# Infini-attention with an adaLN and a bilinear MLP: where ScalarE's bf16 copies, feature maps and high copies stand among the exponentials

## The chip, the cores and the metric

The kernel runs on one core of a Trainium2 chip. The metric is the device time of one execution in microseconds (us). Five engines work side by side, each on a queue of its own and in the order of that queue: TensorE (PE; its weight loads are listed apart as PEld), VectorE (DVE), ScalarE (ACT), GpSimd (POOL) and SyncE (SP), which issues the DMA transfers. An engine that waits for another holds up everything queued behind the waiting instruction.

## The reference

The input x has 2048 rows of 512. It is normed and modulated, goes through attention with 32 heads of 16 in four segments of 512 rows, is added back, and then goes through a second norm and a gated MLP of width 1376. Per segment:

```python
logits = einsum("bhqd,bhkd->bhqk", qs, ks) * scale + mask     # causal inside the segment
p = softmax(logits);  a_dot = einsum("bhqk,bhkd->bhqd", p, vs)
pq = phi(qs)                        # phi(t) = t + 1 where t > 0, exp(t) elsewhere
num = einsum("bhld,bhde->bhle", pq, M);  den = einsum("bhld,bhd->bhl", pq, z) + 1e-6
o = g * num / den + (1 - g) * a_dot
pk = phi(ks)
M = M + einsum("bhld,bhle->bhde", pk, vs);  z = z + pk.sum over l

x = x + ga * (o @ wo)
h = layernorm(x) * (1 + cb) + sb
x = x + gb * (((h @ w_gate) * (h @ w_up)) @ w_down)
```

All arithmetic is fp32. `sa, ca, ga, sb, cb, gb` come from silu(c) @ w_mod.

## The kernel before

**Stages.** A setup of some 45 us loads weights and makes the first segment's norm, k, q and v. The attention loop runs from about 45 to 545 us. The MLP stage takes the rest.

**Splitting for fp32.** Most products are made of three fp32r matmuls over a high and a low part of each operand: `wqH`, `wqL`, `ahH`, `ahL` and so on. A norm's output tile `hf` (in the profile `ahf` for the attention's norm, `chf` for the MLP's) is evicted from a PSUM bank by ScalarE (L183), ScalarE copies it into the high part (`ahH`, `chH`, L190) and POOL subtracts to get the low part (`ahL`, `chL`, L191). For the attention `hf` has two buffers, for the MLP one. The raw scores are made in bf16: k and q are cut into three bf16 parts (`q3`; in the profile `k` and `q`). Part 0 is a ScalarE copy (L657) with POOL's remainder `kr` or `qr` (L658); part 1 is a ScalarE cast of that remainder (L661), after which POOL makes part 2 (L662) and SyncE writes all parts to DRAM (`kd`, `qd`, L665 and L668), from where `load` reads them into `kst` and `qst`.

**The loop.** It steps over 32 units `v`, each of one segment, one of four groups of eight heads, and one half of the group: `u = s*8 + g*2 + half`. Five slots make a unit. A slot does this on TensorE, in this order: `q_step`, the raw scores of a coming unit into bank "lq", whose row maximum VectorE takes (`mxb`); pieces of the unit before, `av_step` (p times v) in slot 1 and `t_step` (transpose back, divide, add the memory's part into `orow`) in slot 4; `fill`, a share of background work; and `k_step`, the transposed scores into bank "lk", which ScalarE empties with one exponential into `pt` (L311), and POOL masks (L314). "lq" and "lk" have one buffer each, so the next `k_step` waits for the exponential before.

**Background work** is written as generators that yield after each piece. `fill_a` makes the coming segment: `ln` and the projections `a_kq` and `a_v`; `a_mem` is the memory's read and update of a group. `fill_b`, in the last segment, makes the output projection of the finished segments (`wo_op`: transposes `op`, high part `oH` by ScalarE, L421, low part `oL` by VectorE) and the MLP's first norm (`lnC`). `fill(share)` draws pieces from them until a credit of time is used up.

**a_kq** ends with the feature map phi, which is written as min(exp, 1) + relu: ScalarE makes `rl` (L681) and `e` (L682; `phk`, `phq` in the profile), and VectorE joins them in one min-and-add, which is put into the list `later` and issued by `flush()` in the next slot. `a_mem` transposes `phk` (bank `mp`, evicted as `pkr`, L720) and multiplies `phq` with the memory MZ (bank `up`, evicted as `us`, L731). `mp`, `up`, `mz` and `tr` share one bank, "sm".

**What sets the order.** TensorE's order is that of the program text: each matmul is chained behind the one before by a dependence without a semaphore. VectorE's instructions in the loop are chained in the same way. ScalarE, POOL and SyncE are ordered by the scheduler of the framework, which places each instruction as the program's dependences and its own model of time allow.

Of the kernel before, what the change touches and what calls it, by code (L numbers as in the profile page):

```python
# [57 lines left out]
def tile_kernel(ctx, tc, x, wq, wk_, wv, wo, beta, w_gate, w_up, w_down, c, w_mod, out):  # L58
    nc = tc.nc
# [19 lines left out]
    def pin(i):  # L79

        if last_pe[0] is not None:
            tc.add_manual_dep(i.ins, last_pe[0].ins.name, NOSYNC, reason="order")
# [4 lines left out]
    def TP(*a):  # L87
        return pe(nc.tensor.transpose(*a))
# [51 lines left out]

    def ln(pool, hpool, xt, s, sc, sh, pfx, hb, fast):

        first = pfx == "a" and s == 0
        V, A = (CV, CA) if first else (vec, act)
        mv = pool.tile([P, 4, 2], F32, tag="mv", name=f"{pfx}mv{s}", bufs=2)
        for t in range(4):
            st = pool.tile([P, 6], F32, tag="st", name=f"{pfx}st{s}_{t}", bufs=2)
            i = V.bn_stats(st, xt[t])  # L150
            if not first:
                pin(i)
            V.bn_aggr(mv[:, t, :], st)  # L153
            if not first:
                yield 0.0
        sd = pool.tile([P, 4], F32, tag="sd", name=f"{pfx}sd{s}", bufs=2)
        A.activation(sd, mv[:, :, 1], AF.Ln, bias=epst[:, 0:1])
        y = pool.tile([P, 4], F32, tag="y", name=f"{pfx}y{s}", bufs=2)
        A.activation(y, sd, AF.Exp, scale=-0.5)
        a = pool.tile([P, 4], F32, tag="ya", name=f"{pfx}ya{s}", bufs=2)  # L160
        b = pool.tile([P, 4], F32, tag="yb", name=f"{pfx}yb{s}", bufs=2)
        eng = CV if first else nc.gpsimd
        eng.tensor_mul(a, y, y)
        eng.tensor_scalar(b, mv[:, :, 1], 1.0, EPS, op0=ALU.mult, op1=ALU.add)  # L164
        eng.tensor_mul(b, b, a)
        eng.tensor_scalar(b, b, -0.5, 1.5, op0=ALU.mult, op1=ALU.add)
        eng.tensor_mul(y, y, b)
        yield 0.0
        for t in range(4):
            i = V.tensor_scalar(xt[t], xt[t], mv[:, t, 0:1], y[:, t:t + 1],  # L170
                                op0=ALU.subtract, op1=ALU.mult)
            if not first:
                pin(i)
                yield 0.0
        if first:
            yield 0.0
        hH, hL = [], []
        for d in range(KT):
            ps = bank(f"{pfx}tp{s}_{d}")
            for t in range(4):  # L180
                TP(ps[:, t * P:(t + 1) * P], xt[t][:, d * P:(d + 1) * P], ident)
            h = pool.tile([P, L], F32, tag="hf", name=f"{pfx}hf{s}_{d}", bufs=hb[2])
            A.activation(h, ps, AF.Identity, scale=sc[:, d:d + 1], bias=sh[:, d:d + 1])  # L183
            hi = hpool.tile([P, L], F32R, tag=hb[0].format(d), name=f"{pfx}hH{s}_{d}", bufs=hb[1])
            lo = hpool.tile([P, L], F32R, tag=hb[0].format(4 + d), name=f"{pfx}hL{s}_{d}", bufs=hb[1])
            if fast:
                V.tensor_copy(hi, h)
                V.tensor_sub(lo, h, hi.bitcast(F32))
            else:
                act.activation(hi, h, AF.Copy)  # L190
                nc.gpsimd.tensor_sub(lo, h, hi.bitcast(F32))  # L191
            hH.append(hi)
            hL.append(lo)
            yield 0.45
            if not first and d % 2 == 1:
                yield False
        return hH, hL

    def run(gen):
# [93 lines left out]
    def k_step(u, i):  # L293

        Q, K = qst[u % NB], kst[u % NB]
        kp = psp.tile([P, 2, 512], F32, tag="lk", name=f"k{u}_{i}", bufs=1)

        def mm(b, c, h, kb):
            MM(kp[:, b, c:c + L - kb * P], K[:, h, kb * P:(kb + 1) * P], Q[:, h, kb * P:], start=True, stop=True)

        for b in range(2):
            if i < 2:
                mm(b, 0, 2 * i + b, 0)
            elif i < 4:
                mm(b, 0, 2 * i - 4 + b, 1)
                mm(b, 384, 2 * i - 4 + b, 3)
            else:
                mm(b, 0, 2 * b, 2)
                mm(b, 256, 2 * b + 1, 2)
        pt = ap.tile([P, 2, 512], F32, tag="pt", name=f"pt{u}_{i}", bufs=PT)  # L310
        act.activation(pt, kp, AF.Exp, scale=0.25)  # L311
        v = pt.rearrange("p b (j t) -> p (b j) t", t=P)
        for w in ((v[:, 0:8:4],) if i < 2 else (v[:, 0:8:4], v[:, 3:8:4]) if i < 4 else (v[:, 0:8:2],)):
            sels[u, i] = nc.gpsimd.affine_select(w, w, pattern=[[0, w.shape[1]], [1, P]], compare_op=ALU.is_ge,  # L314
                                                 fill=0.0, base=0, channel_multiplier=-1)
        ptiles[u, i] = pt
# [308 lines left out]
            yield 0.68  # L625

    done = set()
    later = []

    def flush():  # L630

# [5 lines left out]
    def a_kq(s, g, nm):  # L637

        hH, hL = hcur[0]
        ph = phs.setdefault((s, g), {})  # L640
        if True:
            dst = kd if nm == "k" else qd
            ps = bank(f"{nm}ps{s}_{g}")
            n = 0
            for k in range(KT):
                for a, b in ((wH, hH), (wL, hH), (wH, hL)):
                    MM(ps, a[nm, g][:, k, :], b[k], start=n == 0, stop=n == 11)
                    n += 1
                    if n in (3, 6, 9):
                        yield 0.68  # L650
            f = pa.tile([P, L], F32, tag="f", name=f"{nm}f{s}_{g}", bufs=2)
            fast = s == 0 and g == 0
            A, V = (CA, CV) if fast else (act, nc.gpsimd)
            A.activation(f, ps, AF.Copy)
            q3 = pa.tile([P, 3, L], BF, tag="q3", name=f"{nm}3_{s}_{g}", bufs=2)
            r = pa.tile([P, L], F32, tag="qr", name=f"{nm}r_{s}_{g}", bufs=2)
            A.activation(q3[:, 0, :], f, AF.Copy)  # L657
            V.tensor_sub(r, f, q3[:, 0, :])  # L658

            def rest():  # L660
                (CV.tensor_copy if fast else act.copy)(q3[:, 1, :], r)  # L661
                V.tensor_sub(q3[:, 2, :], r, q3[:, 1, :])  # L662
                for r0, n, k in ((0, 3, 0), (3, 2, 0), (5, 1, 0)) if nm == "k" else ((0, 1, 3), (3, 1, 2), (5, 1, 1)):
                    if nm == "k":
                        nc.sync.dma_start(dst[s][g][r0:r0 + n].rearrange("r p t -> p r t"), q3[:, 0:n, :])  # L665
                    else:
                        i = 3 - k
                        nc.sync.dma_start(dst[s][g][r0:r0 + k].rearrange("r p t -> p r t"),  # L668
                                          q3[:, i:i + 1, :].to_broadcast([P, k, L]))

            if fast:
                rest()
            phi = (nm == "k" and s < NSEG - 1) or (nm == "q" and s > 0)
            if phi:
                if fast:
                    yield 0.0
                if nm == "q" and g > 0:
                    yield from drain()
                e = pa.tile([P, L], F32, tag="ph", name=f"ph{nm}{s}_{g}", bufs=3)
                rl = pa.tile([P, L], F32, tag="rl", name=f"rl{nm}{s}_{g}", bufs=1)  # L680
                act.activation(rl, f, AF.Relu)  # L681
                act.activation(e, f, AF.Exp)  # L682
                ph[nm] = e
            yield 0.68
            if not fast:
                rest()
            if phi:
                later.append(lambda: pin(vec.scalar_tensor_tensor(e, e, 1.0, rl, op0=ALU.min, op1=ALU.add)))
                if fast:
                    flush()  # L690
        nkq[s, g] = nkq.get((s, g), 0) + 1
        if nkq[s, g] == 2:
            done.add((s, g))
# [10 lines left out]
    def drain():  # L704
        while memq:
            w = mem_step()
            if w is not None:
                yield w

    def a_mem(s, g):  # L710

        ph = phs.pop((s, g))
        yield 0.0
        flush()
        if s < NSEG - 1:
            mp = pst((P, 512), "sm", f"mp{s}_{g}")
# [203 lines left out]
    run(av)  # L920
    btag[:] = ["ms"]
    vec.eng = CV
    share = (0.25, 0.0, 0.25, 0.25, 0.25)
    for v in range(-2, NQ + 1):
        rate[0] = 5.5
        on, prev = 0 <= v < NQ, 0 <= v - 1 < NQ
        for slot in range(5):
# [31 lines left out]
            fill(share[slot], slot < 4)  # L959
            if on:  # L960
                k_step(v, slot)
            if slot == 2 and 0 <= v + 1 < NQ:
                n_step(v + 1)
            if slot == 1 and 2 <= v + 3 < NQ:
                until((v + 3) // 8, (v + 3) // 2 % 4)
                load(v + 3)
    btag[:] = ["ms", "tb", "ms", "lk"]
    ps3 = [bank(f"wops3_{t}", shape=(P, 512)) for t in range(4)]
    for t in range(4):
# [98 lines left out]
```

## Time and profile before

| | us |
|---|---|
| median of 3 runs | 934.5 (934.47 to 936.42) |
| profiled execution, own time | 936.69 |
| its span | 934.9 |
| TensorE busy | 901.8 (96%) |
| VectorE busy | 470.9 (50%) |
| ScalarE busy | 409.1 (44%) |
| POOL busy | 313.6 (34%) |

The profiled execution's granted TensorE clock was 0.986 on average. Busy shares are averages over stages with different limits: in the MLP stage VectorE and ScalarE have little to do, and in the attention loop they are well occupied. The page's first lines give busy time by engine, its fourth part the chain of work that ended last, its fifth the costliest groups of instructions with the mean duration of one and the idle time before them. In the timeline a line has the start, the duration, the engine, the source line, the operation with its output and inputs, and in brackets the idle time before it and what ended that.

### The profile page before, as it was taken

To read this page: it belongs to the slowest core of one execution; us is meant where nothing else is said; L and a number is where in the kernel's file an instruction comes from. 1 tells how busy PE (TensorE), PEld (TensorE's weight loads), DVE (VectorE), ACT (ScalarE), POOL (GpSimd) and SP (SyncE) were. 2 spreads that over 40 slices of the span, in tenths; PEclk is the share of its full clock that TensorE was granted. 3 is DMA by queue.
4 is the path that set the end of the run, shared out by engine and by line. 5 is a ranking of instruction groups with operands and counts; after the bars stand their busy time and mean duration, and the time that the engine had idled before them with its cause. 6 is when DMAs were issued, how large, how long until landed. Compare 5 with 4: busy or idle time off the path is not lost.

```text
span 934.9 us, 14252 instructions
## 1 busy us (share of the span) xinstructions
PE 901.8 (96%) x5527; PEld 654.7 (70%) x5528; DVE 470.9 (50%) x758; ACT 409.1 (44%) x603; POOL 313.6 (34%) x455
## 2 busy tenths in 40 slices
PE   8998999999999999998999899999999999999997
PEld 6765666666666666665666668887888788878886
DVE  7577656686566856566667334652233223312112
ACT  3567757687576865577345612231112111211111
POOL 3175535566554763456414514551000000000000
PEclk8999999999999999999899999999999999999999
DMA  6584534655537543566762244440201020101011
GB/s 211 172 253 145 168 114 131 195 171 161 159 92 214 165 142 97 166 207 216 224 200 69 90 137 135 124 116 12 91 1 45 1 90 1 46 0 46 1 46 45
DMA packets 86211, 109.80 MB, mean 117 GB/s; under 512 B 9504, under 2 KB 58656, under 8 KB 86144
## 3 DMA queue, kind: packets, MB, share of 16 engines
q1 hardware_dynamic: 86000, 108.89, 37.6%
q8 instruction: 43, 0.70, 0.3%
q14 instruction: 24, 0.20, 0.1%
q10 hardware_dynamic: 144, 0.02, 0.0%
HBM read 67.98 MB, written 40.63 MB: 116 GB/s over the span
## 4 chain that ended last, share of the span: by engine, by line
PE 84%; DVE 6%; ACT 4%; DMA 3%; issue 1%; POOL 1%; DVEq 0%; SPq 0%; ACTq 0%
PE gps L1004 13%; PE ups L1004 13%; PE q L85 9%; PE tb L85 7%; PE k L85 7%; PE wops L85 5%; PE kps L85 4%; PE vps L85 4%; PE qps L85 3%; DVE mxb L39 2%; ACT pt L311 2%; PE acc0lq L1025 2%; PE acc2lq L1025 2%; PE acc3lq L1025 2%; PE acc1lq L1025 2%; PE acc1lk L1025 2%
## 5 line engine op out<-in xcount | busy, mean ns | idle before, releaser
L39 DVE TENSOR_REDUCE mxb<-q 128x8 f32<-128x1024 f32 x160 | 195.4, 1221 | 133.8 <-PE q L85 133.7
L311 ACT ACTIVATE pt<-k 128x1024 f32<-128x1024 f32 x160 | 163.6, 1022 | 81.0 <-PE k L85 79.6
L314 POOL TENSOR_SCALAR_AFFINE_SELECT pt<-pt 128x256 f32<-128x256 f32 (+1 forms) x224 | 98.9, 455 | 185.0 <-ACT pt L311 182.8
L1009 DVE TENSOR_TENSOR gs<-gs,ups 128x512 f32<-128x512 f32 (+1 forms) x44 | 30.2, 687 | 194.1 <-PE ups L1004 194.1
L85 PE MATMUL k<-qst,kst 98*128 98x384 bf16 (+3 forms) x512 | 98.0, 304 | 7.8 <-ACT pt L311 7.6
L85 PE MATMUL q<-kst,qst 96*128 96x128 bf16 (+2 forms) x640 | 96.7, 273 | 3.6 <-DVE mxb L39 2.3
L1008 ACT ACTIVATE gs<-gps 128x512 f32<-128x512 f32 (+1 forms) x44 | 26.1, 596 | 146.5 <-PE gps L1004 146.5
L1012 ACT ACTIVATE mH<-gs 128x512 fp32r<-128x512 f32 (+1 forms) x44 | 27.8, 633 | 130.5 <-DVE gs L1009 127.0
L85 PE MATMUL tb<-pt,v 128*32 128x512 f32 (+3 forms) x1024 | 75.5, 436 | 0.0
L85 PEld LDWEIGHTS <-kst 98*128 98x128 bf16 x512 | 38.5, 99 | 50.0 <-issue 44.3
L85 PEld LDWEIGHTS <-qst 96*128 96x128 bf16 x640 | 52.9, 98 | 28.1 <-issue 8.2
L1004 PE MATMUL gps<-chH,gH 128*128 128x512 f32 (+1 forms) x176 | 69.4, 394 | 0.0
L1004 PE MATMUL gps<-chH,gL 128*128 128x512 f32 (+1 forms) x176 | 69.3, 394 | 0.0
L1004 PE MATMUL ups<-chH,uH 128*128 128x512 f32 (+1 forms) x176 | 69.3, 394 | 0.0
L1004 PE MATMUL ups<-chL,uH 128*128 128x512 f32 (+1 forms) x176 | 69.3, 394 | 0.0
L1004 PE MATMUL gps<-chL,gH 128*128 128x512 f32 (+1 forms) x176 | 69.3, 394 | 0.0
L1004 PE MATMUL ups<-chH,uL 128*128 128x512 f32 (+1 forms) x176 | 69.2, 393 | 0.0
L85 PEld LDWEIGHTS tb<-pt,v 128*32 128x32 f32 x1024 | 28.7, 110 | 45.0 <-issue 40.4
L85 PE MATMUL q<-cmask,identb 128*128 128x128 bf16 (+1 forms) x320 | 54.6, 252 | 0.0
L164 POOL TENSOR_SCALAR cyb<-cmv 128x4 f32<-128x4 f32 x4 | 1.1, 275 | 143.5 <-DVE cmv L153 142.6
L1013 DVE TENSOR_TENSOR mL<-gs,mH 128x512 fp32r<-128x512 f32 (+1 forms) x44 | 31.7, 720 | 28.7 <-ACT mH L1012 28.5
L85 PEld LDWEIGHTS <-identb 128*128 128x128 bf16 x320 | 30.0, 98 | 17.2 <-issue 0.6
(267 smaller groups left out, 1843.8 us busy)
## 6 DMA issues: line engine op xcount, KB each, us to landing
kst<-kd SPq DMA_DIRECT2D x32, 384.0 KB, 4.5
qst<-qd SPq DMA_DIRECT2D x32, 384.0 KB, 5.2
wm<-in_w_mod_dram SPq DMA_DIRECT2D x24, 256.0 KB, 5.8
kd<-k SPq DMA_DIRECT2D x16, 384.0 KB, 4.1
qd<-q SPq DMA_DIRECT2D x16, 384.0 KB, 2.8
x<-in_x_dram SPq DMA_DIRECT2D x16, 256.0 KB, 4.9
kd<-k SPq DMA_DIRECT2D x16, 256.0 KB, 3.5
qd<-q SPq DMA_DIRECT2D x16, 256.0 KB, 3.7
```

The costliest lines, as they stand in the source:

```text
L39: i = getattr(self.eng, name)(*a, **k)
L85: return pe(nc.tensor.matmul(*a, **k))
L164: eng.tensor_scalar(b, mv[:, :, 1], 1.0, EPS, op0=ALU.mult, op1=ALU.add)
L311: act.activation(pt, kp, AF.Exp, scale=0.25)
L314: sels[u, i] = nc.gpsimd.affine_select(w, w, pattern=[[0, w.shape[1]], [1, P]], compare_op=ALU.is_ge, fill=0.0, base=0, channel_multiplier=-1)
L1004: nc.tensor.matmul(ps[0:n], a[:, k, 0:n], b[k], start=j == 0, stop=j == 11)
L1008: act.activation(gs[0:n], pss[0][0:n], AF.Copy)
L1009: vec.tensor_mul(gs[0:n], gs[0:n], pss[1][0:n])
L1012: act.activation(mH[0:n], gs[0:n], AF.Copy)
L1013: vec.tensor_sub(mL[0:n], gs[0:n], mH[0:n].bitcast(F32))
L1025: nc.tensor.matmul(acc[t], a[0:n, t * P:(t + 1) * P], b[0:n, :], start=i == 0 and j == 0, stop=i == NF - 1 and j == 2)
```

## The change

Inside the loop, ScalarE's instructions that empty no PSUM bank are no longer issued where the program text makes them. They become small functions in a queue `kept`: the high copy of a norm with POOL's subtraction (`parts`), part 0 of the bf16 parts with POOL's remainder (`part0`), the Relu (`phi0`), part 1 with POOL's part 2 and the writes to DRAM (`part1`), and the feature map's exponential (`phi1`), which also puts VectorE's min-and-add into `later`. After each slot's `k_step`, `give(2)` issues two of them, or three if more wait, each with a dependence (no semaphore) behind the slot's exponential, so that ScalarE's order has the exponential first. The whole queue is issued ahead of an eviction of `kf` or `qf`, ahead of a norm's eviction where more than one waits, at the end of a norm, ahead of each `load`, and at the end of the loop. `a_mem` issues one after another until the feature maps that it reads are made (`made`). In `a_kq` the draining of the memory's work moves ahead of the Relu. Outside the loop, and for the first group, all is issued at once as before.

```diff
+    kept, looped, lpt = [], [False], [None]
+    def keep(f):
+        if looped[0]:
+            kept.append(f)
+        else:
+            f()
+    def behind(i):
+        if lpt[0] is not None:
+            tc.add_manual_dep(i.ins, lpt[0].ins.name, NOSYNC, reason="order")
+        return i
+    def give(n=None):
+        n = len(kept) if n is None else n + (len(kept) > n + 1)
+        for _ in range(min(n, len(kept))):
+            kept.pop(0)()
...
     def ln(pool, hpool, xt, s, sc, sh, pfx, hb, fast):
...
+            if len(kept) > 1:
+                give()
             h = pool.tile([P, L], F32, tag="hf", name=f"{pfx}hf{s}_{d}", bufs=hb[2])
             A.activation(h, ps, AF.Identity, scale=sc[:, d:d + 1], bias=sh[:, d:d + 1])
...
-                act.activation(hi, h, AF.Copy)
-                nc.gpsimd.tensor_sub(lo, h, hi.bitcast(F32))
+                def parts(hi=hi, lo=lo, h=h):
+                    behind(act.activation(hi, h, AF.Copy))
+                    nc.gpsimd.tensor_sub(lo, h, hi.bitcast(F32))
+                keep(parts)
...
+        give()
         return hH, hL
...
     def k_step(u, i):
-        act.activation(pt, kp, AF.Exp, scale=0.25)
+        lpt[0] = act.activation(pt, kp, AF.Exp, scale=0.25)
...
     def a_kq(s, g, nm):
+            give()
             f = pa.tile([P, L], F32, tag="f", name=f"{nm}f{s}_{g}", bufs=2)
...
-            A.activation(q3[:, 0, :], f, AF.Copy)
-            V.tensor_sub(r, f, q3[:, 0, :])
+            def part0():
+                behind(A.activation(q3[:, 0, :], f, AF.Copy))
+                V.tensor_sub(r, f, q3[:, 0, :])
-            def rest():
-                (CV.tensor_copy if fast else act.copy)(q3[:, 1, :], r)
+            def part1():
+                if fast:
+                    CV.tensor_copy(q3[:, 1, :], r)
+                else:
+                    behind(act.copy(q3[:, 1, :], r))
                 V.tensor_sub(q3[:, 2, :], r, q3[:, 1, :])
...
+            if not fast:
+                keep(part0)
+            if phi and not fast and nm == "q" and g > 0:
+                yield from drain()
...
+            def phi0():
+                behind(act.activation(rl, f, AF.Relu))
+            def phi1():
+                behind(act.activation(e, f, AF.Exp))
+                made.add((s, g, nm))
+                later.append(lambda: pin(vec.scalar_tensor_tensor(e, e, 1.0, rl, op0=ALU.min, op1=ALU.add)))
...
+                for x in (phi0, part1, phi1) if phi else (part1,):
+                    keep(x)
...
     def a_mem(s, g):
+        while kept and any((s, g, nm) not in made for nm in ph):
+            give(1)
         flush()
...
+    looped[0] = True
     for v in range(-2, NQ + 1):
...
             if on:
                 k_step(v, slot)
+            give(2)
...
                 until((v + 3) // 8, (v + 3) // 2 % 4)
+                give()
                 load(v + 3)
+    give()
+    flush()
+    looped[0] = False
```

More of the change, by code (lines that the diff above doesn't have):

```diff
@@ L627, in tile_kernel @@
     done = set()
-    later = []
+    later, made = [], set()
     def flush():
@@ L669, in rest @@
                                           q3[:, i:i + 1, :].to_broadcast([P, k, L]))
-            if fast:
-                rest()
             phi = (nm == "k" and s < NSEG - 1) or (nm == "q" and s > 0)
+            if not fast:
+                keep(part0)
+            if phi and not fast and nm == "q" and g > 0:
+                yield from drain()
+            e = rl = None
             if phi:
[L675 to L678, printed above, removed]
                 e = pa.tile([P, L], F32, tag="ph", name=f"ph{nm}{s}_{g}", bufs=3)
                 rl = pa.tile([P, L], F32, tag="rl", name=f"rl{nm}{s}_{g}", bufs=1)
-                act.activation(rl, f, AF.Relu)
-                act.activation(e, f, AF.Exp)
-                ph[nm] = e
[L684 to L690, printed above, removed]
+            def phi0():
[4 more added lines that the diff above has]
+                later.append(lambda: pin(vec.scalar_tensor_tensor(e, e, 1.0, rl, op0=ALU.min, op1=ALU.add)))
+            if fast:
+                part0()
+                part1()
+                yield 0.0
+                if phi:
+                    phi0()
+                    phi1()
+                    flush()
+                yield 0.68
+            else:
+                for x in (phi0, part1, phi1) if phi else (part1,):
+                    keep(x)
+                if phi:
+                    ph[nm] = e
+                yield 0.68
+            if fast and phi:
+                ph[nm] = e
         nkq[s, g] = nkq.get((s, g), 0) + 1
@@ L965, in tile_kernel @@
                 until((v + 3) // 8, (v + 3) // 2 % 4)
+                give()
                 load(v + 3)
+    give()
+    flush()
+    looped[0] = False
     btag[:] = ["ms", "tb", "ms", "lk"]
```

## The prediction

> **What bounds the kernel now.** I read the page first: the span, then the chain that ended last.
>
> ```profile
> span 934.9 us, 14252 instructions
> ...
> PE 84%; DVE 6%; ACT 4%; DMA 3%; issue 1%; POOL 1%; DVEq 0%; SPq 0%; ACTq 0%
> ```
>
> TensorE (PE) carries 84% of the chain. ScalarE (ACT) carries 4%, and that small share is what the change can touch. So the question is where TensorE stands still because an exponential came late. The view of windows, over the attention loop (columns: stretch; length; busy time of PE, its weight loads, VectorE, ScalarE, POOL, each with its count; granted clock; DMA share; GB/s):
>
> ```profile
> 45.00:545.00 500.00, 476.20 (x3667) 314.26 (x3664) 320.18 (x492) 320.34 (x458) 259.86 (x379) 0.99 0.52 161
> ```
>
> TensorE is busy 476.20 of 500 us; all its idle time together is 23.8 us. ScalarE is busy 64% of the loop, so it has room on average, and order within a slot is all that can matter. The groups and the waits name the piece:
>
> ```profile
> L311 ACT ACTIVATE pt<-k 128x1024 f32<-128x1024 f32 x160 | 163.6, 1022 | 81.0 <-PE k L85 79.6
> ...
> PE k L85 <- ACT pt L311: 7.6, 12, 1.2
> ```
>
> There are 160 exponentials of 1.022 us. They usually wait for TensorE (79.6 us); TensorE waits for them 12 times, 7.6 us in all, because the bank "lk" that the exponential empties has one buffer. 7.6 us of 934.9 is the ceiling of what the change can give there: 0.8%. In about half of the twelve no deferrable part stands in front of the exponential, so the change cannot touch them; the four places below hold the rest.
>
> **The change, part by part: gains.** I compared the order of instructions on each engine before and after. TensorE's own order does not change. On ScalarE some forty exponentials go ahead of parts, but only where TensorE waited is that time. From the timeline (start, duration, engine; in brackets the idle time before and who ended it):
>
> ```profile
> 72.80 0.61 ACT L682 ACTIVATE phk<-kf 128x512 f32<-128x512 f32 x1
> 73.32 1.00 ACT L311 ACTIVATE pt<-k 128x1024 f32<-128x1024 f32 x1
> ...
> 74.37 0.59 PE L85 MATMUL k<-qst,kst 98*128 98x512 bf16 x2 [0.47 <-ACT pt L311]
> ...
> 90.53 0.63 ACT L190 ACTIVATE ahH<-ahf 128x512 fp32r<-128x512 f32 x1
> 91.07 1.00 ACT L311 ACTIVATE pt<-k 128x1024 f32<-128x1024 f32 x1
> ...
> 92.13 0.59 PE L85 MATMUL k<-qst,kst 98*128 98x512 bf16 x2 [0.57 <-ACT pt L311]
> ```
>
> At 73 us the exponential stood behind the 0.61 us feature map `phk`; in the new order it goes first, and the 0.47 us goes: take 0.5. At 91 us it stood behind the 0.63 us high copy `ahH`, which now follows it; of 0.57 I take 0.5.
>
> ```profile
> 204.21 0.60 PE L85 MATMUL k<-qst,kst 98*128 98x384 bf16 x4 [1.22 <-ACT pt L311]
> ...
> 206.27 1.45 ACT L183 ACTIVATE ahf<-atp,modc 128x512 f32<-128x512 f32 x2 [0.40 <-PE atp L88]
> ...
> 209.20 0.59 PE L85 MATMUL k<-qst,kst 98*128 98x512 bf16 x2 [0.66 <-ACT pt L311]
> ```
>
> At 201 to 209 us the waits are larger, 1.22 and 0.66, yet ScalarE itself is nearly full: its one gap in the stretch is 0.40, ahead of the evictions `ahf`. The new order puts the Relu, the exponential of the feature map and the second bf16 part (0.6 us each, as `phk` above) between the next exponential and those evictions, and the evictions free the banks for the transposes that follow. What the k matmul gains, the transposes hand back. Between 0 and 1.22 + 0.66 = 1.88 I take 0.2, below the 0.40 of slack.
>
> ```profile
> 330.96 1.45 ACT L183 ACTIVATE ahf<-atp,modc 128x512 f32<-128x512 f32 x2
> ...
> 332.82 1.02 ACT L311 ACTIVATE pt<-k 128x1024 f32<-128x1024 f32 x1
> 333.72 0.60 ACT L720 ACTIVATE pkr<-mp 128x512 f32<-128x512 f32 x1
> 333.89 0.60 PE L85 MATMUL k<-qst,kst 98*128 98x384 bf16 x4 [1.17 <-ACT pt L311]
> ...
> 334.98 0.45 PE L85 MATMUL up<-MZ,phq 128*128 128x136 f32 x2
> ```
>
> At 333 us the exponential loses the second eviction and a high copy in front, so the 1.17 us could go. What is late next is `pkr`: `up` needs the bank that `pkr` empties, `pkr` ends at 334.32 at the soonest (333.72 + 0.60), and `up`, moved up by 1.17, would want to start at 334.98 - 1.17 = 333.81. So 334.98 - 334.32 = 0.66 at most stays; I take 0.5. The gains sum to 0.5 + 0.5 + 0.2 + 0.5 = 1.7 us; in full as recorded the four places would give 0.47 + 0.57 + 1.88 + 1.17 = 4.1.
>
> **Losses.** The parts that move back feed POOL and VectorE, and these run in their own queues, where the late part finds something else in front. There are three places where TensorE then waits. First:
>
> ```profile
> 388.70 1.18 POOL L658 TENSOR_TENSOR kr<-kf,k 128x512 f32<-128x512 f32 x1
> 389.82 0.42 POOL L314 TENSOR_SCALAR_AFFINE_SELECT pt<-pt 128x256 f32<-128x256 f32 x1
> 389.92 0.62 ACT L661 CAST k<-kr 128x512 bf16<-128x512 f32 x1 [2.35 <-POOL kr L658]
> ```
>
> Here POOL's remainder `kr` comes behind one more select in the new order. ScalarE already stood 2.35 us for `kr` with the exponential queued behind the cast, so 0.42 more on POOL is 0.42 more for that exponential and the k matmul behind it: loss 0.4, from 0 to 0.42.
>
> The last of these lines is the group that the first belongs to (busy time, then mean ns of one).
>
> ```profile
> 426.01 0.68 DVE L39 SCALAR_TENSOR_TENSOR phq<-phq,rlq 128x512 f32<-128x512 f32 x1
> ...
> 427.71 1.22 DVE L39 TENSOR_REDUCE mxb<-q 128x8 f32<-128x1024 f32 x1 [0.18 <-PE q L85]
> ...
> 428.26 0.63 PE L85 MATMUL up<-MZ,phq 128*128 128x136 f32 x4
> 428.43 1.27 POOL L366 TENSOR_TENSOR orow<-orow,memb 128x512 f32<-128x512 f32 x1
> ...
> L39 DVE SCALAR_TENSOR_TENSOR phq<-phq,rlq 128x512 f32<-128x512 f32 x12 | 11.4, 949 | 0.0
> ```
>
> Second, the last unit's feature map: VectorE's min-and-add was done 1.57 us before `up` reads it at 428.26. In the new order it stands behind one more row maximum, the one at 427.71. It then ends at 427.71 + 1.22 + 0.68 = 429.61, and `up`, and all of TensorE behind it, starts 429.61 - 428.26 = 1.35 late. With the group's mean of 0.949 instead of 0.68 it is 1.62. The bound above is that VectorE starts only when POOL's addition to `orow` ends, at 429.70: 429.70 + 0.68 - 428.26 = 2.1. The bound below is 0, should VectorE find the part before that maximum. I take 1.35, since the part's own row says 0.68. A group whose mean lies 0.27 above this row's 0.68 fits a VectorE that is sometimes held. The Trainium skill (SBUF — State Buffer, section "SBUF: two separate sides") says that VectorE and GpSimd share one pair of ports, and that an operation of VectorE with two operands in SBUF against one of GpSimd that reads SBUF waits for the whole other instruction; by it the loss here is the 2.1 and the net of the sum 0.8 worse, and that mean above 0.68 is on its side.
>
> Third, the layer norm of the first MLP segment, which runs inside the last units. Its float tile `chf` has one buffer, so its links follow one another:
>
> ```profile
> 509.41 0.63 ACT L190 ACTIVATE chH<-chf 128x512 fp32r<-128x512 f32 x1
> 510.13 1.26 POOL L191 TENSOR_TENSOR chL<-chf,chH 128x512 fp32r<-128x512 f32 x1 [1.02 <-ACT chH L190]
> 510.62 1.02 ACT L311 ACTIVATE pt<-k 128x1024 f32<-128x1024 f32 x1 [0.58 <-PE k L85]
> 511.54 0.77 ACT L183 ACTIVATE chf<-ctp,modc 128x512 f32<-128x512 f32 x1
> ...
> 516.67 0.60 PE L88 MATMUL op<-ident,orl 128*128 128x128 f32 x4
> ...
> 518.16 0.78 ACT L183 ACTIVATE chf<-ctp,modc 128x512 f32<-128x512 f32 x1
> 518.30 0.69 DVE L39 TENSOR_TENSOR oL<-op,oH 128x512 fp32r<-128x512 f32 x1 [0.84 <-ACT oH L421]
> ...
> 518.99 0.83 PE L88 MATMUL op<-ident,orl 128*128 128x128 f32 x4 [1.72 <-ACT chf L183]
> ```
>
> The high copy `chH` moves from 509.41 to behind the exponential of 510.62, to 511.54, where the next `chf` starts now: 2.13 later. POOL's `chL` and the next `chf` wait for it in turn, so that `chf` starts at 511.54 + 2.13 = 513.67. Its copy, `chL` and the third `chf` take 0.77 + 0.63 + 1.26 + 0.78 = 3.44, to 517.1 without any further queueing. The changed kernel makes the first `op` transposes wait for that third `chf`: 517.1 against 516.67, 0.45 late or a little more. The second `op` no longer waits for the fourth `chf`, which was its 1.72 us; its bank is now the one that `oL` reads, and `oL` ended at 518.30 + 0.69 = 518.99, the same moment. So it moves with the first, plus what `oH` waits behind an exponential. I take 1.0 in all, between 0 (`oL` comes earlier now that ScalarE is free of that eviction) and 2.1 (the whole shift). The losses sum to 0.4 + 1.35 + 1.0 = 2.75.
>
> **Edits costed at nothing.** The bf16 remainders, and the writes of kd and qd on SyncE's queue that hang on them, come up to a slot later. Ahead of a load all queued parts are given out, so a load never passes its write.
>
> ```profile
> qst<-qd SPq DMA_DIRECT2D x32, 384.0 KB, 5.2
> ...
> 405.81 0.33 SPq L235 DMA_DIRECT2D qst<-qd  x1
> ...
> 418.88 0.38 PE L85 MATMUL q<-kst,qst 96*128 96x512 bf16 x1
> ```
>
> A load lands after 5.2 us and is read 418.88 - 405.81 = 13.1 us after its issue. That leaves 7.9 us of cover; without it the late write's delay, one exponential and a part, would be paid per unit. The MLP stage runs outside the loop and keeps its order: nothing.
>
> **The sum.** +2.75 - 1.7 = +1.05 us, made against the profiled execution: 936.7 of its own time, 934.9 of span and 1.8 around it. That execution lies 2.2 above the median of the runs shown, 934.5. The difference carries over: forecast 935.5. A measurement can tell about 0.2% from no change, 1.9 us, so this is "same".
>
> **Rivals.** Faster: the recorded waits come back in full, and the layer norm costs nothing since `op` is rid of its 1.72 us wait. Then 0.4 + 1.35 - 4.1 = -2.35, so 932.2; with the min-and-add early as well, 930.8. For it speaks that a mere change of order frees ScalarE at the exact places of the waits; against it that 206.27 shows only 0.40 of slack there.
>
> Slower: the parts that feed POOL and VectorE are the bound. The layer norm's one buffer passes its whole 2.1 on and the min-and-add waits for POOL, 2.1: 0.4 + 2.1 + 2.1 - 1.7 = +2.9, so 937.4. It decides for "slower" once these two cost 3.2 together, as 1.9 + 1.7 - 0.4 = 3.2. For it speaks `chf` with its 1.72 us wait already; against it that this wait's bank changes.
>
> The clock: the new waits fall together at 516 to 520 us.
>
> ```profile
> 517.00:520.00 3.00, 1.28 (x9) 0.80 (x8) 1.12 (x3) 2.70 (x5) 2.00 (x4) 0.89 0.07 10
> 520.00:523.00 3.00, 3.00 (x17) 2.81 (x16) 1.54 (x4) 2.06 (x3) 2.08 (x4) 0.54 0.85 315
> ```
>
> After 3 us in which TensorE was busy 1.28, the granted clock was 0.54 for the next 3 us: 3 x 0.46 = 1.4 us lost. Another such stretch, at 428 us say, gives 935.5 + 1.4 = 936.9. The Trainium skill (TensorE: Matmul & The Clock Gate, section "What's actually happening") has the clock halved after one idle window of about 3.4 us; by it the estimate is 1.7 us for a window, and the trace, which lost the clock with TensorE partly busy, bears it out only roughly.
>
> No effect: ScalarE's exponentials go first but every place is covered elsewhere: 934.5.
>
> **How the numbers follow.** Forecast 0.34 (own range 933.2 to 936.8, by the bounds of the two larger losses); faster 0.28; slower 0.25; the clock 0.08; no effect 0.05. Of the forecast's 0.34 I put 0.05 above +1.9. So slower is 0.25 + 0.08 + 0.05 = 0.38, the same 0.29 + 0.05 = 0.34, faster 0.28. As both signs hold much of the chance, the range reaches from near the faster case's end, 931.0, to the slower case with a part of the clock's price, 938.5.
>
> **What would show it.** The waits of k on pt should fall from 12 and 7.6 us to about 8 and 4 to 5, without one at 73, 92 and 333 us. `up` near 428 should wait for VectorE by 1 to 2 us, and `op` near 517 for `chf`, then for `oL`. If k's waits fall by less than 1.7 the gains were mis-sized; if new waits on POOL's remainders or on q and k loads appear elsewhere, a place was missed; a stretch at half clock near 428 or 392 decides for the clock.

## The result and the profile after

The changed kernel is slower, by 0.36%: a median of 938.4 us over 20 runs (935.7 to 943.2) against 935.3 for the kernel before over 20 runs of its own (932.75 to 938.4). The ratio is 1.0036, with a 95% interval of 1.0023 to 1.0049. The forecast was +1.05 us and "same"; the measured +3.1 to +3.4 us is outside what was called the same.

The page of the kernel after, span and chain:

```profile
span 938.3 us, 14251 instructions
...
PE 84%; DVE 9%; ACT 3%; DMA 2%; issue 1%; POOL 0%; SPq 0%; DVEq 0%; ACTq 0%
```

ScalarE's share of the chain fell from 4% to 3%, VectorE's rose from 6% to 9%. The waits show it in detail (who waited for whom: us in all, times, longest). First the kernel before, groups that the prediction did not quote:

```profile
PE op L88 <- DVE oL L39: 3.5, 3, 1.6
PE q L85 <- DVE mxb L39: 2.3, 4, 1.3
PE wops L85 <- DVE oL L39: 2.3, 3, 1.7
PE atp L88 <- DVE x L39: 2.0, 2, 1.0
...
PE mz L85 <- DVE orow L39: 0.4, 1, 0.4
```

and the kernel after:

```profile
PE op L88 <- DVE oL L39: 5.5, 4, 2.0
PE q L85 <- DVE mxb L39: 3.8, 9, 1.3
PE k L85 <- ACT pt L335: 3.4, 7, 1.2
PE atp L88 <- DVE x L39: 3.1, 3, 1.1
...
PE up L85 <- DVE phq L39: 1.4, 1, 1.4
...
PE mz L85 <- DVE orow L39: 1.0, 2, 0.7
...
PE wops L85 <- DVE oL L39: 0.6, 2, 0.4
```

k's waits for the exponential fell from 7.6 us to 3.4, by 4.2, and op's 1.7 us wait for `chf` shrank to a short one. In their place came op on `oL` (+2.0), q on `mxb` (+1.5), `up` on `phq` (+1.4), `atp` on `x` (+1.1) and `mz` on `orow` (+0.6): 6.6 us, all of them waits for VectorE. One wait for VectorE shrank, that of `wops` (the output projection's matmul) for `oL`, by 1.7.

The offset of the same TensorE instruction between the two traces (its start after minus its start before) shows where the 3.3 us of span arose. It is +0.80 at 43 us, before any queued part is issued; +1.24 at 390 us; +1.16 at 425 us and +2.74 at the `up` of 428 us; +1.73 at 451 us; +3.33 at the `wops` behind 523 us, where it stays to the end. So the first 350 us of the loop, with all four places of the predicted gain, brought +0.4 and no gain. The two late places brought +1.6 each. Between them, at 445 us, 1.0 came back, where TensorE had waited in the kernel before:

```profile
445.68 0.79 PE L85 MATMUL wops<-woH,oH 128*128 128x512 f32 x1 [1.73 <-DVE oL L39]
```

This is no gain of the change. The traces of late_now, last_now, ln_clean and before_fold below gain 0.8 to 1.4 us on the trace of before there too, and before_fold is the kernel before without one small product. The wait was long in this one execution of before.

### The profile page after: what moved, and what is told of

Read it like the earlier page. It is cut to its first block, busy times and chain, and to the rows that moved or that the text cites. A ratio compares the mean times of both kernels' runs of the same rounds, so it can differ in the third digit from the quotient of the medians.

```text
span 938.3 us, 14251 instructions
## 1 busy us (share of the span) xinstructions
PE 904.8 (96%) x5528; PEld 656.3 (70%) x5528; DVE 471.6 (50%) x758; ACT 407.8 (43%) x603; POOL 313.8 (33%) x455
## 4 chain that ended last, share of the span: by engine, by line
PE 84%; DVE 9%; ACT 3%; DMA 2%; issue 1%; POOL 0%; SPq 0%; DVEq 0%; ACTq 0%
PE ups L1057 13%; PE gps L1057 13%; PE q L85 9%; PE tb L85 7%; PE k L85 6%; PE wops L85 4%; DVE mxb L39 4%; PE vps L85 4%; PE kps L85 4%; PE qps L85 3%; PE acc2lq L1078 2%; PE acc0lq L1078 2%; PE acc3lq L1078 2%; PE acc1lq L1078 2%; PE acc1lk L1078 2%; PE acc0lk L1078 2%
## 5 line engine op out<-in xcount | busy, mean ns | idle before, releaser
L338 POOL TENSOR_SCALAR_AFFINE_SELECT pt<-pt 128x256 f32<-128x256 f32 (+1 forms) x224 | 96.8, 446 | 185.8 <-ACT pt L335 184.4
```

## The clock, and how the runs are compared

The +0.8 at the start is in the setup, which the change does not touch. These are windows of before and then of after (the granted clock is the third number from the right):

```profile
11.00:25.00 14.00, 13.93 (x67) 12.36 (x69) 11.53 (x25) 6.26 (x8) 0.00 (x0) 0.63 0.63 195
```

```profile
11.00:25.00 14.00, 14.00 (x61) 12.39 (x60) 9.42 (x21) 5.11 (x7) 0.00 (x0) 0.51 0.55 170
```

In the setup the clock was granted at half for 10.2 us in the one execution and 13.7 in the other, and in the execution of kq_only below for none. The mean clock varies from run to run of one kernel, and the time with it: the 20 runs of after lie near a line from 935.7 us at a mean clock of 0.992 to 943.2 at 0.979, and 80 runs of before near one from 930.2 at 0.998 to 938.0 at 0.982, about 0.4 to 0.6 us for each 0.001. Differences of 1 us drown in that. So beside each ratio I give the time at a clock of 0.986, read from a straight line through the kernel's own runs. It is a working of mine and good to about 1 us; for the kernels without `rd` and for those with halved row maxima, six runs each, it reads the line beyond all or most of their clocks. It also has a weakness: the mean clock holds the half-clock stretches that a change itself makes, so a part of their price is taken out. By it before is at 935.2 and after at 938.3: +3.0.

## Experiments

**Undoing the late places together.** Theory: the loss is the two late places, and the gains are handed back. Rival: bad luck with the clock, or a loss spread over the loop. In late_now these parts are issued at once:

```diff
-                keep(parts)
+                keep(parts, pfx == "c")
...
-                keep(part0)
+                keep(part0, last)
...
-                    keep(x)
+                    keep(x, last)
```

with `last = s == NSEG - 1 and g == NG - 1`, and `keep(f, now)` calling `f` at once where `now` holds.

> As after, but the parts of the last segment's last group and of the MLP's norm are issued at once. Theory A: the two late places are gone (1.5 us at 428 us, 1.7 us at 517 to 523 us), everything earlier stays as in after; 935.2, equal to before within 0.5 us, with k's waits on pt still at some 4 us instead of 7.6. Theory B or a loss spread over the loop: still 937.5 to 938.4.

Measured: 936.4, ratio 1.0010 (0.9994 to 1.0026), that is +0.9 us and between -0.6 and +2.4; at equal clock 935.3, 0.0 from before. Its waits:

```profile
PE q L85 <- DVE mxb L39: 3.5, 9, 1.3
PE op L88 <- DVE oL L39: 3.5, 3, 1.6
PE k L85 <- ACT pt L335: 3.2, 7, 1.0
PE atp L88 <- DVE x L39: 3.1, 3, 1.1
PE op L88 <- ACT chf L204: 1.7, 1, 1.7
```

The waits at the two places are those of before again, and k still waits only 3.2 us instead of 7.6: 4.4 us of k's waits are gone, and the time is not below that of before. The clock as the cause of the whole loss falls: the twelve runs of late_now had the same mean clock as those of after, 0.985, and were 2.0 us shorter by the medians, 2.4 by the ratios and 3.0 at equal clock.

**Undoing each by itself**, last_now and c_now, each with one half of that edit.

> As after, but the parts of the last segment's last group are issued at once; the MLP's norm stays queued. Theory: the wait of up on phq (1.4 us) goes, the op waits near 519 us stay: 936.9, 1.5 us below after and 1.6 above before. If the late places are worth nothing alone: 938.4.

> As after, but the MLP's norm issues its high copies at once; the last group stays queued. Theory: the op place costs what it costs before (1.7 us for chf and none for the second bank), up at 428 us still waits 1.4 us: 936.9 to 937.4, 1.0 to 1.5 us below after. If that place is covered (as ln_clean's 934.6 suggests): 938.4, level with after.

Measured: last_now 937.7, ratio 1.0041 (1.0022 to 1.0061), at equal clock 937.3; c_now 937.2, 1.0027 (1.0008 to 1.0045), at equal clock 937.4. By ratio last_now is a miss, no better than after, and c_now is 0.8 us below it; by equal clock each is about 1 us below after's 938.3. Their traces are plainer: in last_now `up` comes 1.4 us earlier than in after and never waits; in c_now the op place is back to 1.7 us and the half-clock stretch behind it ends 3.4 us sooner. c_now's waits on k, q, `atp` and `up` are those of after within 0.3 us. The intervals don't separate 1.0 from 1.5 us, so the size of each place alone rests on the traces, and on late_now for their sum.

**Queueing one kind of part.** kq_only calls `parts()` at once in the norms; ln_only calls the parts of a_kq at once. One piece of the edit of ln_only:

```diff
-                for x in (phi0, part1, phi1) if phi else (part1,):
-                    keep(x)
+                for x in (phi0, phi1, part1) if phi else (part1,):
+                    x()
```

> Only the bf16 parts and feature maps are queued; the norms' high copies are issued at once, as before the change. Theory A: the op waits near 519 us are again those of before, up at 428 us still waits 1.4 us for VectorE; 936.6, 1.3 us above before. Theory C (the norm's parts are the whole loss): at or below before, 934.5 to 935.3. A rival that puts all on the bf16 parts: 938.4.

> Only the norms' high copies are queued; the bf16 parts and feature maps are issued at once, as before the change. Theory A (two late places, gains handed back to VectorE): the wait of up at 428 us goes (1.4 us less than after), the waits of op near 519 us with the longer half-clock stretch stay; 936.8, that is 1.5 us above before. Theory B (the clock was unlucky in after's runs, no place of the change is at fault): within 0.5 us of before, as would kq_only. Theory C (the norm's parts, with their one buffer, are the whole loss): as slow as after, 938.4.

kq_only: 936.8, ratio 1.0017 (1.0001 to 1.0032), at equal clock 937.1; expected 936.6. ln_only: 945.2, ratio 1.0111 (1.0091 to 1.0132), where 936.8 was expected. This was a miss of the experiment, not of the norm: calling `phi1` at once puts VectorE's min-and-add into `later` a slot earlier than in either kernel, and VectorE then stands in its fixed order for a feature map that ScalarE has not made. The groups of ln_only in the loop (after the second bar the idle time before them, and who ended it):

```profile
L39 DVE SCALAR_TENSOR_TENSOR phq<-phq,rlq 128x512 f32<-128x512 f32 x12 | 11.2, 936 | 3.5 <-ACT phq L714 3.5
...
L39 DVE SCALAR_TENSOR_TENSOR phk<-phk,rlk 128x512 f32<-128x512 f32 x11 | 10.4, 943 | 7.6 <-ACT phk L714 7.6
```

and one line of its waits:

```profile
PE q L85 <- DVE mxb L39: 6.3, 10, 2.4
```

VectorE idles 11.1 us there, 0.3 to 0.4 in after, and q's wait for the row maxima behind it grows to 6.3 us. ln_clean repairs that: part 1 and the min-and-add stand where they stood before the change.

```diff
+                    phi0()
+                    act.activation(e, f, AF.Exp)
+                    ph[nm] = e
+                yield 0.68
+                part1()
+                if phi:
+                    made.add((s, g, nm))
+                    later.append(...)
```

> Only the norms' high copies are queued; the bf16 parts, the feature maps and VectorE's min-and-add are issued at the same points as before the change (ln_only gave the min-and-add to VectorE a slot earlier). Theory A: up at 428 us does not wait, the op waits near 519 us are those of after; 936.5. If the 10 us of ln_only belong to queueing the high copies: 945.

Measured: 934.6, ratio 1.0002 (0.9987 to 1.0017); at equal clock 935.2. The 10 us are gone, and the runs are 1.9 us better than the 936.5 expected (1.3 at equal clock). The op place has the waits of after:

```profile
511.85 0.85 PE L88 MATMUL op<-ident,orl 128*128 128x128 f32 x4 [0.54 <-ACT chf L204]
514.50 1.11 PE L88 MATMUL op<-ident,orl 128*128 128x128 f32 x4 [1.80 <-DVE oL L39]
```

Against before, a wait of 0.54 is added and 1.72 becomes 1.80, and the offset to before grows there by 1.7 us, as in after. The runs show no such loss: +0.2 us, between -1.2 and +1.6. Why they came out below what the trace shows is open. k's waits on pt are still 7.0 us in its loop: with the norms alone queued hardly any gain is made, and hardly any is handed back.

**What takes the gains back?** In two places of the trace of after VectorE is held by POOL where it was not, or less, before. At 178 us, in before:

```profile
177.14 0.17 DVE L39 TENSOR_TENSOR rd<-rd,omg 128x16 f32<-128x16 f32 x1
177.17 1.16 POOL L662 TENSOR_TENSOR k<-kr,k 128x512 bf16<-128x512 f32 x1
```

and in after:

```profile
177.11 1.28 POOL L692 TENSOR_TENSOR k<-kr,k 128x512 bf16<-128x512 f32 x1 [0.27 <-ACT k L691]
...
177.59 0.84 DVE L39 TENSOR_TENSOR rd<-rd,omg 128x16 f32<-128x16 f32 x1
...
178.46 0.42 DVE L39 TENSOR_TENSOR orow<-tr,rd 128x256 f32<-128x256 f32 x1
...
179.03 0.93 PE L85 MATMUL mz<-v,pkr 128*128 128x136 f32 x6 [0.70 <-DVE orow L39]
```

The same product of 128x16 takes 0.84 us instead of 0.17; it ends at 178.43, just behind POOL's part 2, which ends at 178.39. In before the product began 0.03 us ahead of part 2 and was not held; in after part 2 is first, since it comes no later than in before, and VectorE reaches the product 0.45 us later. `orow` follows, and TensorE's `mz`, which needs its bank, waits 0.70. The Trainium skill (SBUF — State Buffer, "SBUF: two separate sides") states this very hold for an operation of VectorE with two operands in SBUF beside one of GpSimd that reads SBUF: the one that starts first has the shared ports for its whole length. These starts and ends agree with it. So do the others in the two traces: 11 of these products took more than 0.25 us in before and 15 in after, and each of them ended 0.03 us behind an instruction of POOL. To take the victim away, the inverse of the factor (1-g) was put into the ones column of v, set once, so that the reciprocal gives the scaled value and the product goes:

```diff
+        nc.gpsimd.tensor_copy(a[:, 0:H * VS].rearrange("p (h e) -> p h e", e=VS)[:, :, DH], iom)
...
+        nc.gpsimd.tensor_mul(hmg[:, g, :, DH], hmg[:, g, :, DH], omg[:, g * HG:(g + 1) * HG])
...
         vec.reciprocal(rd, tr[:, :, :, DH])
-        og = omg[:, g * HG + h0:g * HG + h0 + 4]
-        vec.tensor_mul(rd, rd, og.unsqueeze(1).to_broadcast([P, 4, 4]))
```

> As after, with the factor (1-g) moved from VectorE's small product rd into the ones column of v (set once), so that the product with two operands in SBUF goes: 31 operations with a mean of 0.58 us leave VectorE. Theory A with VectorE held by POOL as the taker of the gains: the waits of mz on orow (1.0 us) and part of those of atp on x (3.1 us) and of q on mxb (3.8 us) go; 936.2, 2.2 us below after. Rival (rd's held time is off the path): 938.4, within 0.5 us of after.

> As before, with the factor (1-g) folded into the ones column of v, so that VectorE's product rd goes. Theory A (VectorE and POOL holding each other lies on the path, more so after the change): in before 1.1 us of TensorE's waits are for orow, so the gain is small here, 1.0 us; 934.3 beside 935.3. Rival (the fold is worth the same in both kernels, it has nothing to do with the change): 2.7 us or more below before, as the fold brought in after.

> As after, with both takers undone: the parts of the last group and of the MLP's norm are issued at once, and rd is folded away. Theory A: the two effects add up, 2.0 (late_now against after) + 2.7 (after_fold against after) = 4.7 us below after: 933.7, some 1 to 1.5 us below before and no slower than before_fold. Rival (the gains in k's waits are never real, since VectorE's row maxima pace the loop): level with before_fold or above it.

Measured: after_fold 934.8, ratio 1.0007 (0.9988 to 1.0025), by the ratios 2.7 us below after, where 2.2 were expected. But before_fold is at 930.1, ratio 0.9944 (0.9929 to 0.9959): the fold is worth 5.2 us by ratio (4.5 at equal clock) where I had said 1.0. late_fold is at 929.8, 0.9947 (0.9931 to 0.9962), level with before_fold. So the part of my theory that made this hold the special taker of the change's gains falls: the fold helps before more than after. `rd`'s groups, before and after, show that it was long in both:

```profile
L39 DVE TENSOR_TENSOR rd<-rd,omg 128x16 f32<-128x16 f32 x31 | 15.1, 486 | 1.1
```

```profile
L39 DVE TENSOR_TENSOR rd<-rd,omg 128x16 f32<-128x16 f32 x31 | 18.0, 580 | 1.1
```

The change added 2.9 us to 15.1; 31 products of 0.17 us would be 5.4. And without the product the gains still don't appear: before_fold has 8.4 us of k's waits in the loop and late_fold 3.4, in equal time. First before_fold, then late_fold:

```profile
PE k L85 <- ACT pt L310: 8.4, 13, 1.2
...
PE q L85 <- DVE mxb L39: 1.8, 2, 1.3
```

```profile
PE q L85 <- DVE mxb L39: 4.0, 9, 1.3
...
PE k L85 <- ACT pt L334: 3.4, 8, 1.0
```

5.0 us of k's waits went, and 2.2 us of waits of q for the row maxima came, on 7 more occasions. What is left of the 5.0 does not show in the medians, which are good to about 1 us. That gave the next theory: VectorE's row maxima take the gains. At 73 us, in after:

```profile
74.15 1.19 DVE L39 TENSOR_REDUCE mxb<-q 128x8 f32<-128x1024 f32 x1
...
74.50 0.61 PE L85 MATMUL k<-qst,kst 98*128 98x512 bf16 x2
...
75.39 0.61 PE L85 MATMUL q<-kst,qst 96*128 96x128 bf16 x8 [0.29 <-DVE mxb L39]
```

k no longer waits, and the q behind it does, because bank "lq" is still being read until 75.34. Halving the columns that a row maximum reads (a softmax keeps its value under another maximum) tests this:

```diff
-        vec.tensor_reduce(o, src, axis=AX.X, op=ALU.max)
+        vec.tensor_reduce(o, src[:, :, :, 0:64], axis=AX.X, op=ALU.max)
```

> As before, but each row maximum reads only the first half of each block of 128 columns (the other half is left out of the maximum), so that VectorE's 160 reductions last some 0.7 us instead of 1.22. Theory A' (the four gains are handed back because TensorE, once it need not wait for an exponential, stands at the next q matmul for VectorE's row maximum): waits of q on mxb (2.3 us) go, k's waits on pt stay at 7 us or grow; 932, 2 us below before.

> As after, with the halved row maxima. Theory A': the waits of q on mxb (3.8 us) go, up at 428 us waits 0.5 us less, the op place stays; 932.5, 5 to 6 us below after, and level with before_half because the two late places still cost what the gains bring. Rival (the handing back does not hang on the row maxima): 3 us above before_half, as after is above before.

> As late_now, with the halved row maxima. Theory A': the gains of k's waits show at last: 929.5, 2.5 us below before_half. Rival (VectorE's row maxima are not the taker): level with before_half within 1 us, as late_fold was with before_fold.

Measured: before_half 924.3, ratio 0.9899 (0.9870 to 0.9928); after_half 926.3, 0.9914 (0.9888 to 0.9939); late_half 923.7, 0.9877 (0.9851 to 0.9904). The size was missed by far: 0.53 us less in each row maximum is worth some 10 us of time, where 2 were expected. The waits on the maxima alone don't account for it. About half may be the hold by POOL: with shorter maxima VectorE comes to `rd` at other moments, and in before_half it is hardly held, where taking `rd` away had been worth 5.2 us:

```profile
L39 DVE TENSOR_TENSOR rd<-rd,omg 128x16 f32<-128x16 f32 x32 | 6.2, 195 | 1.1
```

No run separates the two. The comparison of the three does not settle the theory either: late_half lies 0.6 us under before_half by medians, where 2.5 were expected and the rival said less than 1; it is 1.7 at equal clock, and the intervals overlap. after_half lies 2.0 above before_half by medians, where the theory said level and the rival 3. The traces decide it place by place. The same place in after_half:

```profile
70.62 0.69 DVE L39 TENSOR_REDUCE mxb<-q 128x8 f32<-128x512 f32 x1
...
71.57 0.61 PE L85 MATMUL k<-qst,kst 98*128 98x512 bf16 x2
72.01 0.61 PE L85 MATMUL q<-kst,qst 96*128 96x128 bf16 x8
```

Here q follows k without a wait, and the 0.6 us that k gained on before_half is still there 70 us later. It is so at every such place. Between 43 and 390 us the offset falls at six k matmuls in either pair of traces. From before to after these gains sum to 4.3 us, and the very next q hands back 2.2 of them. From before_half to after_half they sum to 4.1, and the next q hands back 0.03. So the row maximum is shown as the taker of about half of what k gains.

The rest goes to other queues. At 317 us of after_half `atp` waits 0.8 us for VectorE's `x` where k had gained 0.8, and at 172 us `mz` waits 0.7 for `orow`. From 62 to 390 us after_half gains 1.1 us on before_half, where after loses 0.5 on before. Over the whole loop that gain is not left. At 62 us after_half waits for a load, which before_half does not:

```profile
62.43 0.60 PE L85 MATMUL q<-kst,qst 96*128 96x512 bf16 x2 [1.19 <-DMA qst<-qd]
```

The two late places still cost 1.6 and 1.0 us, and at 445 us a q of after_half alone waits 1.3 for a row maximum.

## Why the prediction was wrong, point by point

**The bound** was read rightly as far as it went: k's waits on pt were what the change could touch, and those at 73, 92 and 333 us went as foreseen. 4.2 us went, more than I counted. A fifth place was missed, at 324 us, where the wait went as well:

```profile
324.33 0.60 PE L85 MATMUL k<-qst,kst 98*128 98x256 bf16 x4 [0.88 <-ACT pt L311]
```

**The gains** are the step that failed: of the 1.7 us forecast 0.7 arrived at the four places, and 1.2 of new waits, which the prediction had at nothing, took that and more, so that nothing is left in the times either (late_now against before, late_fold against before_fold). For the place at 201 us and for `up` at 333 us I asked what is late next; for the two at 73 and 91 us I did not, and booked nearly the whole recorded wait. At 73 us 0.67 us were gained and 0.46 lost again at the very next q; at 91 us 0.66 and 0.63. The instruction behind k on TensorE's queue needs bank "lq", whose reader VectorE was late by nearly as much. At 204 us the 0.2 I left was near: k gained 0.78, q and `atp` took 0.71 of it. At 333 us the 0.5 came in, 1.05 gained, 0.2 lost to the next q and 0.4 to `up`, which waits for `pkr` as foreseen. But eight microseconds before it, behind the missed place of 324 us, a wait came that I had not named:

```profile
325.46 1.06 DVE L39 TENSOR_TENSOR rd<-rd,omg 128x16 f32<-128x16 f32 x1
...
327.48 0.77 PE L88 MATMUL atp<-ident,x 128*128 128x128 f32 x5 [1.12 <-DVE x L39]
```

POOL's remainder `qr`, which the change moved behind an exponential, ran from 325.32 to 326.48 and held `rd`, and `x` and `atp` came late behind it. Here the offset grows by 0.7 us on balance, at 178 us by 0.5. This is the second part of the failed step: under "edits costed at nothing" I asked of the bf16 remainders only whether a load would pass its write, and not whom POOL holds while it makes them. With 0.7 of gains these 1.2 leave the balance of the early places at about +0.4.

**The kr step** (0.4) was not paid by k: at 390 us both traces have the same offset as 30 us before. At 391 us `up` lost 0.2, waiting for a ScalarE eviction, and at 400 us 0.3 came back.

**The min-and-add** (1.35) was right in place, cause and size:

```profile
428.87 1.22 DVE L39 TENSOR_REDUCE mxb<-q 128x8 f32<-128x1024 f32 x1
...
430.00 0.85 DVE L39 SCALAR_TENSOR_TENSOR phq<-phq,rlq 128x512 f32<-128x512 f32 x1
...
431.00 0.70 PE L85 MATMUL up<-MZ,phq 128*128 128x136 f32 x4 [1.43 <-DVE phq L39]
```

It stands behind that maximum, and `up` waits 1.43. The end at 430.85 lies after POOL's `orow` ended at 430.31, so VectorE was held for a part, 0.85 against 0.68, and not until POOL's end and for a full 0.68 more, as the other bound had it.

**The layer norm** (1.0, up to 2.1) was right in its mechanism:

```profile
519.40 0.66 PE L88 MATMUL op<-ident,orl 128*128 128x128 f32 x4 [0.53 <-ACT chf L204]
...
522.04 1.12 PE L88 MATMUL op<-ident,orl 128*128 128x128 f32 x4 [1.99 <-DVE oL L39]
```

0.53 for the first `op` (0.45 said), then 1.99 for `oL` instead of 1.72 for `chf`: the offset, 2.04 ahead of them after two small waits (0.3 together), grew by 1.0 up to 522 us. Then came the rival that I gave 0.08, at this place rather than at 428 us. Windows of before and then of after:

```profile
519.00:523.00 4.00, 4.00 (x21) 3.58 (x22) 1.54 (x4) 2.80 (x4) 2.40 (x4) 0.57 0.68 243
523.00:526.60 3.60, 3.30 (x17) 2.54 (x15) 1.70 (x3) 1.54 (x3) 2.76 (x3) 1.00 0.29 96
```

```profile
519.00:523.00 4.00, 1.61 (x9) 1.32 (x10) 1.16 (x3) 2.84 (x5) 2.00 (x3) 0.62 0.30 82
523.00:526.60 3.60, 3.60 (x19) 3.14 (x18) 1.76 (x5) 2.94 (x5) 1.39 (x3) 0.50 0.54 202
```

In before the half clock ends at 522.7; in after, where TensorE worked only 1.61 of the 4 us, it runs on to 526.8. That is another 0.3 us of offset where it settles (3.05 to 3.33), less than the 1.4 priced, since a part of the half-clock stretch fell on time in which TensorE stood, and a wait of `wops` of 0.3 in before is gone. The longer stretch mostly goes with the queued norm: of the six traces with it five have 6.8 us of half clock there, of the eight without it one, that of late_now.

**The sum.** The losses were forecast at 2.75 us. The two late ones measured 1.6 + 1.6 = 3.2 in the trace, and 2.0 to 3.0 in the runs (after against late_now, by the ways above). With the gains at nothing the forecast would have read 934.5 + 2.75 = 937.2 and "slower". The slower rival named the right places, and that its +2.9 came near is in part luck: it had 4.6 us of losses less 1.7 of gains, and there were about 3 and none. That sum, 937.4, is also where the bounds of the two larger losses lead; the 936.8 that the prediction gave as the end of its own range was wrongly added.

## What to carry to other kernels

A recorded wait is a gain only down to the next instruction's own wait: before booking one, look at what the engine does next and when that one's bank comes free, for a short wait as much as for a long one. Where two engines are each busy two thirds of a loop and both free banks for a third, clearing the queue of the one can turn its waits into waits for the other: here 4.2 us of k's waits for ScalarE went, and 3.2 us of waits of q, `atp` and `mz` for VectorE came, beside the late places. Work that is moved on a third engine, here POOL, can hold one of the two. What is given out late needs a slot to spare before its reader, and the last round of a loop has none: issue those at once.

## What the runs showed of the hardware

A product of VectorE over 128x16 took 0.17 us when it began 0.03 us ahead of a POOL subtraction, and 0.84 when it began behind one, ending 0.03 to 0.04 us after it. It took 0.486 us on average over 31 of them in the kernel before, and folding it into a constant made the kernel before 0.56% faster (0.9944, 0.9929 to 0.9959). That version, before_fold, beats both kernels; with the change and its late places undone (late_fold, 0.9947) no more was measured. Half-clock stretches in the loop came in two lengths in these traces, 3.4 us and 6.8. The setup had 0, 6.8, 10.2 or 13.7 us of half clock in executions of much the same code. All are multiples of 3.41 us, so I cut the 14 traces from the loop on into pieces of 3.41 us in step with their half-clock stretches. The full clock was halved 35 times, 34 of them behind a piece in which TensorE was busy at most 0.53 of the time and once behind one of 0.59; of 3415 full-clock pieces that were followed by full clock only three were below 0.55. The full clock came back only behind pieces busy 0.93 or more.
